# Retention and two expert layers on one core: the first two slots of each layer masked instead of redone behind a branch

## The chip, the cores and the metric

The kernel runs on one core of a Trainium2 chip. The metric is the device time of one execution in microseconds (us); lower is better. Times of a kernel are the median of several runs, beside one profiled execution whose trace is read here. Engines are named as in the profile: PE (TensorE matmuls), DVE (VectorE), ACT (ScalarE), POOL (GpSimd) and SP (the engine that issues most transfers; "SPq" in a row is its queue).

## The reference

Retention (linear attention with decay) over 8 batches, 8 heads, 576 positions, then two layers of experts, each sending each of 4608 rows to one of 8 experts:

```python
ret = scores * Dmat                     # decay mask
x = (ret @ v), rows of 512              # 4608 x 512
# layer 1: normalized logits, argmax; layer 2: x @ w_gate, argmax, and a sigmoid output gate
for e in range(E):
    mask = expert_idx == e
    h = np.maximum(x[mask] @ w1[e], 0.0)           # 512 -> 1024
    out[mask] = gate_w[mask, None] * (h @ w2[e])   # 1024 -> 512
```

## The kernel before, in words

**Buckets and slots.** Each row is scattered by POOL to the bucket of its expert in DRAM (`bk1` for layer 1, `bk2` for layer 2, one stretch of 4608 rows per expert). A layer then goes through *slots* of 128 rows, expert after expert; an expert has at least MIN_SLOTS = 3 slots. `slot_tables` (L155) computes on DVE, from the counts of rows per expert, a table `tix` of integers per slot: where its rows start (Q_START), which weights to fetch next (Q_SRC), whether to fetch them (Q_LD for this layer's next expert, Q_LV for layer 2's first), where to put them (Q_WO), which half of the weight tiles it reads (Q_PO). It also makes `val` and `inv`, masks of the valid rows of each slot. Engines read `tix` into registers with `vload` (L840, a TENSOR_LOAD).

**One slot's work.** `gather` (L846, on SP) loads the 128 rows, `trans_x` (L874 to 876) transposes them on PE and splits them on ACT and DVE into a high and a low part (`xth`, `xtl`), `first` (L885) does 24 matmuls against `w1` (high and low tiles), `relu` (L897, L901), `trans_h` (L909 to 911) transposes and splits the hidden rows, `second` (L921) does 24 matmuls against `w2`, `gated` (L932) scales, and the rows are scattered (L293): in layer 1 to `bk2` after the routing of layer 2 (`trans_g`, `chunk_logits`, `logits` L962, `route2a`, `route2b`), in layer 2 to the output.

**Next weights.** During an expert's slots the next expert's weights come in. `load(s, w)` puts a half of `w1` (w = 1) or `w2` (w = 2), 1 MB, into the tile `raw[w-1]` by a transfer of SP that is carried out only if a register says so (`load_raw`, L332). `step(s, w)` splits `raw` into the high and low weight tiles (`split`: ACT L337, then DVE L338), in the place not in use. In layer 1 `load` issues two transfers into the same tile: this layer's weights, then layer 2's (`v1`, `v2`); the second waits until the first has landed or been skipped.

**The start of a layer.** The table isn't ready when PE could begin. So slots 0 and 1 are taken as expert 0, rows 0 to 255 of its bucket (`load_first`), and run before the table is there (`first(0)`, `first(1, [0, 1])`, ...). If fewer than 256 rows of expert 0 had been scattered by then (`tf`, a flag), the two slots are wrong, and `redo` (in a `tc.Switch` on `fail`, L1051, inside `begin`) fetches the first present expert's weights and does both again. All five engines read the flag (`failed`) and branch. Then `begin` does `load(1, 1)`, `load(1, 2)`, the last masks (`late`), zeroes parts of `bk2` (L309, layer 1 only), `first(1, [3])`, `relu(1)`, `second(0)`, `step(1, 1)`, `load(2, 1)`, `trans_x(2)` and `trans_h(1)`. The program order is written by hand (`manual_schedule`); each engine takes its instructions in that order. From slot 2 on, `period(t, n)` is one slot's program: `step(t-1, 2)`, `load(t, 2)`, `first(t)`, `relu(t)`, `step(t, 1)`, `load(t+1, 1)`, `trans_x(t+1)`, `second(t-1)`, and the rest. A second `Switch`, late in each layer, sets the number of slots.

```python
for case in tc.Switch(fail, 2):     # L1051, in begin
    if case == 1:
        redo(e0)
load(1, 1)
load(1, 2)
```

Of the kernel before, what the change touches and what calls it, by code (L numbers as in the profile page):

```python
# [9 lines left out]
F32 = mybir.dt.float32  # L10
F32R = mybir.dt.float32r
BF16 = mybir.dt.bfloat16
I32 = mybir.dt.int32
# [11 lines left out]
E = 8  # L25
# [4 lines left out]
N_EXACT = NU + E - 1  # L30
NS = NU + E - 1 + (E - 1) * (MIN_SLOTS - 1)
# [26 lines left out]
TI_TOT, TI_E, TI_Q = NQ * NS, NQ * NS + 1, NQ * NS + 2  # L58
NTI = NQ * NS + 3
# [15 lines left out]
def retention_moe_moe(ctx, tc, qh, kth, kh, vh, embT, tau, u1, u2, wg, v1, v2, const, out):  # L75
# [20 lines left out]
    def col(c, n=1):  # L96
# [25 lines left out]
            cp.tile([P, 1], I32, name=f"tf{i}"),  # L122
# [34 lines left out]
    def slot_tables(tab, cum_last, cum_part, psum, seq0):  # L157
# [6 lines left out]
        val, inv, ti, tf = tab  # L164
# [3 lines left out]
        ci, incl, q8, le, y8, t8, t9, pos, cf = (  # L168
            T(n, E, I32 if n == "ci" else F32) for n in "ci incl q8 le y8 t8 t9 pos cf".split()
        )  # L170
        ex, er, ce, nx, loc, sl, r0, sq, jj, nw, f1, pq, hn, rr = (
            T(n, 1, I32 if n == "pq" else F32) for n in "ex er ce nx loc sl r0 sq jj nw f1 pq hn rr".split()
# [6 lines left out]
        def q(i, n=1):  # L179
            return Q[:, i : i + n]  # L180
# [10 lines left out]
        def row(i):  # L191
            return pc[1][:, i * NS : (i + 1) * NS]
# [3 lines left out]
            lambda: ts(out=tf, in0=pc[0][:, E : E + 1], scalar1=float(2 * P), scalar2=None, op0=ALU.is_lt),  # L196
            lambda: ts(out=ci, in0=pc[0][:, :E], scalar1=float(P - 1), scalar2=None, op0=ALU.add),
            lambda: ts(
                out=pos, in0=pc[0][:, :E], scalar1=0.0, scalar2=float(MIN_SLOTS), op0=ALU.is_gt, op1=ALU.mult
            ),  # L200
            lambda: stt(out=y8, in0=pc[0][:, :E], scalar=0.0, in1=iota_n, op0=ALU.is_gt, op1=ALU.mult),
            lambda: ts(out=ci, in0=ci, scalar1=7, scalar2=None, op0=ALU.logical_shift_right),
            lambda: red(out=r0, in_=y8, axis=AX.X, op=ALU.min),
# [4 lines left out]
            lambda: ts(out=r0, in0=r0, scalar1=1000.0, scalar2=float(E - 1), op0=ALU.add, op1=ALU.min),  # L208
            lambda: ts(out=le, in0=incl, scalar1=iota_p, scalar2=0.0, op0=ALU.is_le, op1=ALU.add, accum_out=er),
            lambda: stt(out=q8, in0=incl, scalar=iota_p, in1=incl, op0=ALU.is_le, op1=ALU.mult),  # L210
            lambda: V.tensor_copy(ti[:, TI_E : TI_E + 1], r0[on]),
# [6 lines left out]
            else V.tensor_tensor(out=pq, in0=sq, in1=seq0, op=ALU.add),  # L218
            lambda: stt(
                out=t8, in0=iota_e, scalar=er, in1=pc[0][:, :E], op0=ALU.is_equal, op1=ALU.mult, accum_out=ce  # L220
# [54 lines left out]
            lambda: stt(out=val, in0=row(Q_REM), scalar=iota_p, in1=val, op0=ALU.is_gt, op1=ALU.mult),  # L275
            lambda: ts(out=inv, in0=val, scalar1=-BIG, scalar2=BIG, op0=ALU.mult, op1=ALU.add),
# [3 lines left out]
    def emit(fs):  # L280
        for f in fs:
            f()
# [39 lines left out]
    def load_raw(w, src, ms, cond=None):  # L322

        r = raw[w - 1]
        m = ms[w - 1].rearrange("e k f -> (e k) f")
        if w == 1:
            o, i = r, m[ds(src, 2 * P), :].rearrange("(m p) f -> p m f", p=P)
        else:
            o, i = r.rearrange("p m (j d) -> p m j d", j=2), m[ds(src * 2, 4 * P), :].rearrange(
                "(m j p) d -> p m j d", p=P, j=2  # L330
            )
        nc.sync.dma_start(o, i, **({} if cond is None else {"cond": cond}))  # L332

    def split(w, r, m, off_a, off_v, step):
# [4 lines left out]
        if step:  # L339
            for o in ops:  # L340
                tc.declare_no_dep(o.ins, group="rd", reason="the place written is not the one in use")
                tc.add_to_no_dep_group("wr", o.ins)
        return ops[-1]

    def reads_weights(mm, after=None):

        keep = [after.ins] if after is not None else []
        tc.declare_no_dep(mm.ins, group="wr", keep=keep, reason="the place read is not the one being written")
        if after is not None:
            tc.add_manual_dep(  # L350
                mm.ins,
                after.ins.name,
                mybir.DependencyInfo(mybir.DependencyClass.Sync, mybir.DependencyReason.DATA),
                reason="weights",
            )
        tc.add_to_no_dep_group("rd", mm.ins)
# [467 lines left out]
    def layer(which):  # L824
# [4 lines left out]
        val, inv, ti, tf = tabs[which - 1]  # L829
        ps_h, ps_o, rt, pk, src, po, wo, made = {}, {}, {}, {}, {}, {}, {}, {}  # L830
        L.state = (ps_h, ps_o, rt, pk, src, po, wo, made)
# [12 lines left out]
        def gather(s):  # L844
            r = vload(nc.sync, Q_START * NS + s, E * NT - P)
            nc.sync.dma_start(xrow(s), bk[ds(r, P), :])  # L846

        def load(s, w):

            if w == 1:  # L850
                src[s] = [vload(nc.sync, q * NS + s, mx) for q, mx in ((Q_SRC, E * DM - 2 * P), (Q_LD, 1), (Q_LV, 1))]
            r, ld, lv = src[s]
            load_raw(w, r, ws, ld)
            if g:
                load_raw(w, r, (v1, v2), lv)

        def step(s, w):

            if w == 1:
                wo[s] = [vload(q, Q_WO * NS + s, 3 * FF) for q in (nc.scalar, nc.vector)]  # L860
            for m in range(2):
                made[s, w] = split(w, raw[w - 1], m, *wo[s], True)
# [157 lines left out]
        def start_at(off):  # L1020

            L.base = off if isinstance(off, tuple) else (off,) * 3
            po[0] = po[1] = L.base[2]

        def redo(e0):

            for j in range(2):
                for w in (1, 2):
                    load_raw(w, e0 * DM + j * 2 * P, ws)
                for w in (1, 2):  # L1030
                    for m in range(2):
                        split(w, raw[w - 1], m, L.base[0] + j * FF, L.base[1] + j * FF, False)
            gather(0)
            gather(1)
            trans_x(0, "T", 2)
            first(0)
            relu(0)
            trans_x(1, "T", 2)
            first(1, range(3))
            trans_h(0)  # L1040

        def failed():
            return {e: vload(q, 0, 1, tf) for e, q in everyone.items()}

        def begin(fail, late):


            for s in range(2, 5):
                gather(s)
            e0 = vload(nc.sync, TI_E, E - 1)  # L1050
            for case in tc.Switch(fail, 2):  # L1051
                if case == 1:
                    redo(e0)
            load(1, 1)
            load(1, 2)
# [12 lines left out]
            gated(0)  # L1068
            if not g:
                store(0)  # L1070
            trans_h(1)

        def period(t, n):

            more = g or t < n - 1
            step(t - 1, 2)
            if more:
                load(t, 2)
# [24 lines left out]
            if t + 3 < n:  # L1103
                gather(t + 3)
            if g:
                logits(t - 2)
# [22 lines left out]
        for f in (trans_x, first, relu, trans_h, second, gated, store, trans_g, chunk_logits, logits, route2a, route2b, rank2, failed, begin, run, step, vload, start_at, after):  # L1129
            setattr(L, f.__name__, f)  # L1130
# [28 lines left out]
    fail = L1.failed()  # L1159
    L1.trans_h(0)  # L1160
    emit(tb[ns:-3])
# [4 lines left out]
    for j in range(2):  # L1166
        for m in range(2):
            split(2, raw[j], m, j * FF, j * FF, False)
# [50 lines left out]
    fail = L2.failed()  # L1219
    L2.trans_h(0)  # L1220
    emit(tb[ns:-3])
    L2.first(1, [2])
    L2.begin(fail, tb[-3:])
# [92 lines left out]
```

## Time and profile before

| | us |
|---|---|
| median of 3 runs (1261.49 to 1266.49) | 1264.6 |
| the profiled execution's own time | 1261.13 |
| its span, first to last instruction | 1259.4 |
| PE busy | 1203.2 (96%) |
| DVE busy | 789.4 (63%) |
| ACT busy | 618.5 (49%) |

The span is the stretch that the trace shows; the own time is some 1.7 us longer. A row of the timeline gives start, duration, engine, line, and in brackets the idle time just before it with what ended it. "issue" means that the engine waited for nothing that the profile shows.

### The profile page before, as it was taken

Reading aid. Unit: us, or ns where it says so; the run is one execution under the profiler, and the core shown is the slowest. Engines: PE = TensorE matmul, PEld = TensorE weight load, DVE = VectorE, ACT = ScalarE, POOL = GpSimd, SP = SyncE. Lnnn points to the kernel's source line nnn. Section 1 sums busy time; section 2 is a strip of 40 time slices with the busy share of each in tenths; the row PEclk is TensorE's granted clock in tenths of the full one; section 3 lists DMA queues with packets and bytes.
Section 4 is the critical chain, followed back from the end, with each engine's and each line's share of the span. In section 5 each row is a group of like instructions: output and inputs, shape, how many; then the busy total and the mean of one; then the engine's idle time right before and its main releaser. Section 6 shows DMA issues by size and latency. Waiting matters only on the chain. (4 is left out here: it accounts for less than half of the span.)

```text
span 1259.4 us, 27235 instructions
## 1 busy us (share of the span) xinstructions
PE 1203.2 (96%) x7620; PEld 994.7 (79%) x7620; DVE 789.4 (63%) x1799; ACT 618.5 (49%) x1080; POOL 200.6 (16%) x360
## 2 busy tenths in 40 slices
PE   7998997699999999999999996999999999999997
PEld 6888885588788888888878874888888888888786
DVE  4588675466777667667766764556565655556553
ACT  1454442354555555455555542455555555555453
POOL 3378661000100000010010010000000000000000
PEclk8999997799999999999999998999999999999999
DMA  9997953624343433443443303215144562663110
GB/s 315 269 362 270 329 208 116 178 78 160 112 142 106 157 127 128 142 173 111 166 141 136 123 36 114 100 61 209 59 172 151 200 216 70 213 207 112 35 43 21
DMA packets 89343, 191.02 MB, mean 152 GB/s; under 512 B 9020, under 2 KB 18620, under 8 KB 89152
## 3 DMA queue, kind: packets, MB, share of 16 engines
q1 hardware_dynamic: 78784, 159.16, 38.6%
q0 software_dynamic: 9120, 28.91, 5.8%
q8 instruction: 85, 1.39, 0.5%
q14 instruction: 106, 0.87, 0.2%
q10 hardware_dynamic: 1248, 0.69, 0.2%
HBM read 301.76 MB, written 35.36 MB: 268 GB/s over the span
## 5 line engine op out<-in xcount | busy, mean ns | idle before, releaser
L921 PE MATMUL po<-w2h,hth 128*128 (+1 forms) x624 | 258.4, 414 | 2.4 <-DVE val L275 2.4
L921 PE MATMUL po<-w2h,htl 128*128 (+1 forms) x624 | 247.1, 396 | 0.0
L921 PE MATMUL po<-w2l,hth 128*128 (+1 forms) x624 | 247.0, 396 | 0.0
L338 DVE TENSOR_TENSOR w1l<-raw,w1h 128x1024 f32 x150 | 176.8, 1220 | 83.0 <-ACT w1h L337 83.0
L885 PE MATMUL ph<-w1h,xth 128*128 (+1 forms) x624 | 204.2, 409 | 21.5 <-issue 9.2
L338 DVE TENSOR_TENSOR w2l<-raw,w2h 128x1024 f32 (+1 forms) x154 | 181.7, 1222 | 50.8 <-ACT w2h L337 45.8
L911 DVE TENSOR_TENSOR htl<-pt,hth 128x512 fp32r<-128x512 f32 x156 | 100.5, 686 | 178.1 <-ACT hth L910 177.6
L885 PE MATMUL ph<-w1l,xth 128*128 (+1 forms) x624 | 196.4, 396 | 0.6 <-DVEq L1051 0.6
L885 PE MATMUL ph<-w1h,xtl 128*128 (+1 forms) x624 | 195.0, 394 | 0.0
L337 ACT CAST w1h<-raw 128x1024 f32 x150 | 149.9, 1047 | 63.7 <-DMA raw<-in_v_dram 56.4
L337 ACT CAST w2h<-raw 128x1024 f32 (+1 forms) x154 | 153.9, 1054 | 11.8 <-issue 6.5
L932 ACT ACTIVATE orow<-po,xg 128x512 f32<-128x512 f32 x74 | 50.9, 687 | 195.0 <-PE po L921 192.4
L885 PEld LDWEIGHTS ph<-w1h,xth 128*128 128x128 f32 x624 | 112.8, 192 | 42.6 <-issue 14.7
L921 PEld LDWEIGHTS po<-w2h,hth 128*128 128x128 f32 x624 | 118.3, 190 | 33.4 <-issue 9.7
L885 PEld LDWEIGHTS ph<-w1l,xth 128*128 128x128 f32 x624 | 118.7, 190 | 27.2 <-DVEq L1051 1.3
L921 PEld LDWEIGHTS po<-w2h,htl 128*128 128x128 f32 x624 | 118.0, 189 | 28.1
L885 PEld LDWEIGHTS ph<-w1h,xtl 128*128 128x128 f32 x624 | 118.8, 190 | 26.6
L921 PEld LDWEIGHTS po<-w2l,hth 128*128 128x128 f32 x624 | 118.7, 190 | 22.7
L293 POOL DMA_INDIRECT bk<-orow,bix x39 | 38.2, 980 | 504.9 <-DVE orow L1016 318.2
L897 ACT ACTIVATE hs<-ph 128x512 f32<-128x512 f32 x78 | 46.5, 597 | 132.8 <-PE ph L885 132.8
L293 POOL DMA_INDIRECT out_dram<-orow,oix x39 | 37.9, 972 | 457.6 <-ACT orow L932 425.9
L910 ACT CAST hth<-pt 128x512 fp32r<-128x512 f32 x156 | 83.6, 589 | 8.8 <-PE pt L909 8.8
(205 smaller groups left out, 1398.2 us busy)
## 6 DMA issues: line engine op xcount, KB each, us to landing
raw<-in_v_dram SPq DMA_DIRECT2D x150, 1024.0 KB
raw<-in_w_dram SPq DMA_DIRECT2D x76, 1024.0 KB
xg<-bk SPq DMA_DIRECT2D x74, 264.0 KB
qt<-in_qh_dram SPq DMA_DIRECT2D x36, 256.0 KB
vr<-in_vh_dram SPq DMA_DIRECT2D x36, 256.0 KB
kr<-in_kh_dram SPq DMA_DIRECT2D x36, 256.0 KB
kt<-in_kth_dram SPq DMA_DIRECT2D x34, 256.0 KB
bk<-z SPq DMA_DIRECT2D x18, 264.0 KB
```

The costliest lines, as they stand in the source:

```text
L293: i = nc.gpsimd.indirect_dma_start(out=table, out_offset=bass.IndirectOffsetOnAxis(ap=ix, axis=0), in_=rows, in_offset=None, bounds_check= ...
L337: ops = [nc.scalar.copy(at(h[m], off_a, 0, FF), r[:, m, :])]
L338: ops.append(nc.vector.tensor_sub(at(l[m], off_v, 0, FF), r[:, m, :], at(h[m], off_v, 0, FF)))
L885: mm = nc.tensor.matmul(ps_h[s][i], st[:, k, :], at(w1[n][k % 2], po[s], k // 2 * FF + i * 512, 512), start=(k == 0 and n == 0 and st is x ...
L897: nc.scalar.activation(hsb[:, 0:512], ph[0], AF.Relu)
L910: nc.scalar.copy(hth[s % 2][:, h, :], ps)
L911: nc.vector.tensor_sub(htl[s % 2][:, h, :], ps, hth[s % 2][:, h, :])
L921: mm = nc.tensor.matmul(ps, st[:, f, :], at(w2[n][a % 2], po[s], a // 2 * FF + b * 512, 512), start=(f == 0 and n == 0 and st is hh), stop ...
L932: nc.scalar.activation(o[:, 0:DM], ps_o.pop(s), AF.Copy, scale=x[:, DM : DM + 1])
```

## The change

The branch and `redo` are gone. Instead the number of rows of expert 0 that were missing from the first two slots, d0 = max(0, 256 - count at that time), is computed; `val` masks slots 0 and 1 down to what was there, expert 0's count is raised by d0, and its later slots start d0 rows earlier. Expert 0 gets at least 4 slots instead of 3 (`MIN_SLOTS + 1`), and its fetch of next weights runs one slot later (`lj` for `loc`): `begin` has no `step(1, 1)`, and loads for slot 2 rather than for slot 1. In layer 1 the transfers of layer 2's weights (`load_v`) stand apart from `load`, later in SP's order, and no longer wait for the other transfer into the same tile. The slot table has room for 60 slots instead of 57.

```diff
-            lambda: ts(out=tf, in0=pc[0][:, E : E + 1], scalar1=float(2 * P), scalar2=None, op0=ALU.is_lt),
+            lambda: ts(
+                out=d0, in0=pc[0][:, E : E + 1], scalar1=-1.0, scalar2=float(2 * P), op0=ALU.mult, op1=ALU.add
             ),
+            lambda: ts(out=d0, in0=d0, scalar1=0.0, scalar2=None, op0=ALU.max),
...
+            lambda: ts(out=cf[:, 0:1], in0=cf[:, 0:1], scalar1=float(MIN_SLOTS + 1), scalar2=None, op0=ALU.max),
...
+            lambda: ts(out=lj, in0=er, scalar1=1.0, scalar2=-float(P), op0=ALU.is_lt, op1=ALU.mult),
+            lambda: V.tensor_tensor(out=lj, in0=lj, in1=loc, op=ALU.add),
...
+            lambda: ts(out=val[:, 0:1], in0=iota_p, scalar1=d0, scalar2=float(2 * P), op0=ALU.add, op1=ALU.is_lt),
+            lambda: ts(out=val[:, 1:2], in0=iota_p, scalar1=d0, scalar2=float(P), op0=ALU.add, op1=ALU.is_lt),
...
-            load_raw(w, r, ws, ld)
-            if g:
-                load_raw(w, r, (v1, v2), lv)
+            loads[s, w] = [load_raw(w, src[s][0], ws, src[s][1])]
+
+        def load_v(s, w, apart=True):
+
+
+            got = load_raw(w, src[s][0], (v1, v2), src[s][2])
+            if apart:
+                tc.add_to_no_dep_group("raw", loads[s, w][0].ins)
+                tc.declare_no_dep(got.ins, group="raw", reason="one of the two at most is carried out")
+            loads[s, w].append(got)
...
-        def begin(fail, late):
+        def begin(late):
 
 
             for s in range(2, 5):
                 gather(s)
-            e0 = vload(nc.sync, TI_E, E - 1)
-            for case in tc.Switch(fail, 2):
-                if case == 1:
-                    redo(e0)
-            load(1, 1)
-            load(1, 2)
+            load(2, 1)
+            load(2, 2)
+            if g:
+                load_v(2, 1)
+                load_v(2, 2)
             emit(late)
...
-            step(1, 1)
-            load(2, 1)
             trans_x(2)
...
-            step(t - 1, 2)
-            if more:
-                load(t, 2)
+            if t > 2:
+                step(t - 1, 2)
+                if more:
+                    load(t, 2)
+                    if g and t == n - 1:
+                        load_v(t, 2, False)
...
                 load(t + 1, 1)
+                if g and t > 2:
+                    load_v(t, 2)
...
                 gather(t + 3)
+            if g and t + 1 < n:
+                load_v(t + 1, 1)
...
-    L1.begin(fail, tb[-3:])
-    base2 = tuple(L1.vload(e, TI_Q, 2 * FF) for e in (nc.scalar, nc.vector, nc.tensor))
+    L1.begin(tb[-5:])
+    base2 = L1.vload(nc.tensor, TI_Q, 2 * FF)
```

What moves, in the engines' own order (rows of the compiled program; `raw_74` and `raw_75` are raw[0] and raw[1], `in_w` the layer's weights, `in_v` layer 2's, `xs`, `xg` gathered rows; in brackets the semaphores an instruction waits for).

ACT, layer 1, from the branch's end into slot 1. Before:

```order
L1312 UNCONDITIONAL_BRANCH
L897 ACTIVATE hs<-ph_1_0_3149 128x512 [waits PE_49,Activation_49]
L840 TENSOR_LOAD tix [waits DVE_49]
L840 ISA x2
L337 ISA
L337 COPY w1h_70<-raw_74 128x1024 [waits DMAHW3_49,DVE_49]
L337 ISA
L337 COPY w1h_71<-raw_74 128x1024 [waits DVE_49]
L875 CAST xth_2939<-px_2_3553 128x512 [waits DVE_49,PE_49]
L932 ACTIVATE orow_3263<-po_0_3474,xs_86 128x512 [waits DMASW7_49,DMASW6_49,DMAHW5_49,DMASW3_49,DMAHW6_49,DMASW2_49,PE_49]
L910 CAST hth_2945<-pt_1_0_3568 128x512 [waits PE_49]
```

And now:

```order
L345 CAST w2h_3203<-raw_75 128x1024
L908 ACTIVATE hs<-ph_1_0_3155 128x512 [waits PE_49,Activation_49]
L886 CAST xth_2937<-px_2_3341 128x512 [waits PE_49]
L943 ACTIVATE orow_3224<-po_0_3313,xs_86 128x512 [waits DMASW6_49,DMASW3_49,DMASW7_49,DMASW2_49,DMAHW5_49,DVE_49,PE_49]
L921 CAST hth_2943<-pt_1_0_3356 128x512 [waits PE_49]
L921 CAST hth_2943<-pt_1_1_3363 128x512 [waits PE_49]
L908 ACTIVATE hs<-ph_2_0_3408 128x512 [waits PE_49,Activation_49]
L845 TENSOR_LOAD tix [waits DVE_49]
L845 ISA x2
L345 ISA
L345 COPY w1h_70<-raw_74 128x1024 [waits DMAHW4_49,DMAHW2_49]
```

The split of `w1` from `raw[0]`, which waits for a transfer (DMAHW), stood ahead of `xth`, `orow` and `hth`; now it stands behind them and behind slot 2's `relu`.

SP, layer 1, the loads of `begin`. Before (behind the branch and three `vload`s):

```order
L332 ISA
L332 DMA raw_74<-in_w_dram 128x2x1024 [waits DMAHW2_49,DMAHW4_49,DVE_49,Activation_49]
L332 ISA
L332 DMA raw_74<-in_v_dram 128x2x1024 [waits DMAHW3_49,DMAHW2_49]
L332 ISA
L332 DMA raw_75<-in_w_dram 128x4x512 [waits DMAHW5_49,DVE_49,Activation_49]
L332 ISA
L332 DMA raw_75<-in_v_dram 128x4x512 [waits DMAHW4_49]
L309 DMA bk_69<-z 512x1x132 [waits DMAHW6_49]
```

And now:

```order
L338 ISA
L338 DMA raw_74<-in_w_dram 128x2x1024 [waits DMAHW2_49,DVE_49]
L338 ISA
L338 DMA raw_75<-in_w_dram 128x4x512 [waits DMAHW3_49,DVE_49]
L338 ISA
L338 DMA raw_74<-in_v_dram 128x2x1024 [waits DMAHW4_49]
L338 ISA
L338 DMA raw_75<-in_v_dram 128x4x512 [waits DMAHW5_49]
L315 DMA bk_69<-z 512x1x132 [waits DMAHW6_49]
```

The two `in_w` loads stand next to each other; between them stood the wait of the `in_v` transfer for the first.

SP, layer 1, in the periods. Before, `load(3, 1)` with its `in_v`, `gather(5)`, and `load(3, 2)` with its `in_v`:

```order
L332 ISA
L332 DMA raw_74<-in_w_dram 128x2x1024 [waits DMAHW3_49,DMAHW0_49,DVE_49]
L332 ISA
L332 DMA raw_74<-in_v_dram 128x2x1024 [waits DMAHW4_49,DMAHW3_49]
L840 TENSOR_LOAD tix
L840 ISA x2
L846 ISA
L846 DMA xg_3260<-bk_68 128x528 [waits DMAHW5_49]
L332 ISA
L332 DMA raw_75<-in_w_dram 128x4x512 [waits DMAHW6_49,DMAHW2_49,DVE_49]
L332 ISA
L332 DMA raw_75<-in_v_dram 128x4x512 [waits DMAHW6_49]
```

And now `load(4, 1)`, `load_v(3, 2)`, `gather(6)`, `load_v(4, 1)`, `load(4, 2)`:

```order
L338 ISA
L338 DMA raw_74<-in_w_dram 128x2x1024 [waits DMAHW3_49,DMAHW1_49,DVE_49]
L338 ISA
L338 DMA raw_75<-in_v_dram 128x4x512 [waits DMAHW4_49]
L845 TENSOR_LOAD tix
L845 ISA x2
L851 ISA
L851 DMA xg_3222<-bk_68 128x528 [waits DMAHW5_49,Activation_49,Pool_49]
L338 ISA
L338 DMA raw_74<-in_v_dram 128x2x1024 [waits DMAHW6_49]
L338 ISA
L338 DMA raw_75<-in_w_dram 128x4x512 [waits DMAHW7_49,DMAHW4_49,DVE_49]
```

Each `in_v` transfer now follows its `in_w` at a distance, the one for `raw[1]` about half a period later than it did.

## Rows read from the trace of the kernel before

**Rows 1.** The page: busy time of PE, its share and number of instructions; and the granted TensorE clock in 40 equal slices of the span, in tenths.

```profile
PE 1203.2 (96%) x7620; PEld 994.7 (79%) x7620; DVE 789.4 (63%) x1799; ACT 618.5 (49%) x1080; POOL 200.6 (16%) x360
...
PEclk8999997799999999999999998999999999999999
```

**Rows 2.** The waits of PE over the whole span: who was waited for, us in total, times, longest.

```profile
PE pl L962 <- ACT lsb L959: 9.5, 3, 8.8
PE ph L885 <- issue: 9.2, 2, 5.1
PE ph L885 <- ACT hth L910: 8.6, 2, 5.3
```

**Rows 3.** The timeline of PE at the start of layer 1: start, duration, what, and in brackets the idle time before it.

```profile
199.26 0.63 PE L885 MATMUL ph<-w1h,xtl 128*128 128x512 f32 x2
204.04 1.22 PE L885 MATMUL ph<-w1h,xth 128*128 128x512 f32 x2 [4.16 <-issue]
...
210.39 0.77 PE L921 MATMUL po<-w2h,hth 128*128 128x512 f32 x1 [2.43 <-DVE val L275]
...
216.08 0.43 PE L921 MATMUL po<-w2l,hth 128*128 128x512 f32 x1
...
223.37 1.19 PE L885 MATMUL ph<-w1h,xth 128*128 x2 [3.21 <-ACT hth L910]
...
228.07 0.62 PE L885 MATMUL ph<-w1l,xth 128*128 x2
228.53 0.61 PE L885 MATMUL ph<-w1h,xtl 128*128 x2
...
230.34 0.60 PE L944 MATMUL pg<-ident,orow 128*128 128x128 f32 x4
...
237.11 0.40 PE L921 MATMUL po<-w2h,htl 128*128 128x512 f32 x1
246.28 0.61 PE L962 MATMUL pl<-cs,lsb 128*128 128x16 f32 x2 [8.77 <-ACT lsb L959]
...
248.33 1.20 PE L885 MATMUL ph<-w1h,xth 128*128 x2
...
254.80 0.60 PE L944 MATMUL pg<-ident,orow 128*128 128x128 f32 x4
```

**Rows 4.** The timelines of DVE, ACT and SP's queue in the same stretch (for SP: issue of a transfer; x3 and x9 are merged, with the time from the first to the last issue).

```profile
201.15 4.63 DVE L338 TENSOR_TENSOR w2l<-raw,w2h 128x1024 fp32r<-128x1024 f32 x4
209.66 0.28 DVE L274 TENSOR_SCALAR val<-tabs,cs 128x57 f32<-128x57 f32 x1 [3.88 <-issue]
...
219.79 1.99 ACT L337 CAST w1h<-raw 128x1024 f32 x2 [11.55 <-DMA raw<-in_v_dram]
...
243.59 1.99 ACT L337 CAST w1h<-raw 128x1024 f32 x2 [12.62 <-DMA raw<-in_v_dram]
...
204.41 2.84 SPq L846 DMA_DIRECT2D xg<-bk  x3
214.60 0.41 SPq L332 DMA_DIRECT2D raw<-in_w_dram  x1
219.64 0.10 SPq L332 DMA_DIRECT2D raw<-in_v_dram  x1
...
225.36 8.55 SPq L309 DMA_DIRECT2D bk<-z  x9
236.66 0.39 SPq L332 DMA_DIRECT2D raw<-in_w_dram  x1
243.45 0.08 SPq L332 DMA_DIRECT2D raw<-in_v_dram  x1
```

**Rows 5.** The timelines of PE, DVE, ACT and SP's queue at the start of layer 2.

```profile
769.46 1.22 PE L885 MATMUL ph<-w1h,xth 128*128 x2 [5.06 <-issue]
...
772.18 0.56 PE L921 MATMUL po<-w2h,hth 128*128 x1
...
776.54 0.60 PE L874 MATMUL px<-ident,xg 128*128 128x128 f32 x4
...
784.77 1.19 PE L885 MATMUL ph<-w1h,xth 128*128 x2 [5.35 <-ACT hth L910]
...
792.59 0.60 PE L874 MATMUL px<-ident,xg 128*128 128x128 f32 x4
...
761.10 0.15 DVE L244 TENSOR_TENSOR st_Q<-st_f,st_Q 128x1 f32<-128x1 f32 x1
...
781.18 1.99 ACT L337 CAST w1h<-raw 128x1024 f32 x2 [8.54 <-DMA raw<-in_v_dram]
...
765.66 3.60 SPq L846 DMA_DIRECT2D xg<-bk  x3
776.01 20.89 SPq L332 DMA_DIRECT2D raw<-in_v_dram  x5
```

**Rows 6.** Slots and their length: the page's groups of the first half of `relu` (one per slot run) and of the scatters of layer 1 (one per slot), with busy time, mean ns, idle before; and two gathers of neighbouring slots in SP's timeline.

```profile
L293 POOL DMA_INDIRECT bk<-orow,bix x39 | 38.2, 980 | 504.9 <-DVE orow L1016 318.2
...
L897 ACT ACTIVATE hs<-ph 128x512 f32<-128x512 f32 x78 | 46.5, 597 | 132.8 <-PE ph L885 132.8
...
811.89 0.35 SPq L846 DMA_DIRECT2D xg<-bk  x1
824.27 0.35 SPq L846 DMA_DIRECT2D xg<-bk  x1
```

More of the change, by code (lines that the diff above doesn't have):

```diff
@@ L29 @@
 MIN_SLOTS = 3
[L30 to L31 removed]
+NS = NU + E - 1 + (E - 1) * (MIN_SLOTS - 1) + 3
 BIG = 262144.0
@@ L157, in slot_tables @@
     def slot_tables(tab, cum_last, cum_part, psum, seq0):
-        val, inv, ti, tf = tab
+        val, inv, ti = tab
         V = nc.vector
@@ L167, in slot_tables @@
         T = lambda n, k, dt=F32: cp.tile([P, k], dt, tag="st_" + n, bufs=2, name="st_" + n)
[L168 to L172 removed]
+        ci, incl, q8, le, y8, t8, t9, pos, cf, cc = (
+            T(n, E, I32 if n == "ci" else F32) for n in "ci incl q8 le y8 t8 t9 pos cf cc".split()
+        )
+        ex, er, ce, nx, loc, sl, sq, jj, nw, f1, pq, hn, rr, d0, de, lj = (
+            T(n, 1, I32 if n == "pq" else F32) for n in "ex er ce nx loc sl sq jj nw f1 pq hn rr d0 de lj".split()
         )
@@ L331, in load_raw, with split @@
             )
-        nc.sync.dma_start(o, i, **({} if cond is None else {"cond": cond}))
-    def split(w, r, m, off_a, off_v, step):
+        return nc.sync.dma_start(o, i, cond=cond)
+    SYNC = mybir.DependencyInfo(mybir.DependencyClass.Sync, mybir.DependencyReason.DATA)
+    def split(w, r, m, off_a, off_v, loads=()):
         h, l = (w1, w2)[w - 1]
@@ L338, in split @@
         ops.append(nc.vector.tensor_sub(at(l[m], off_v, 0, FF), r[:, m, :], at(h[m], off_v, 0, FF)))
-        if step:
+        for i in loads:
+            tc.add_manual_dep(ops[0].ins, i.ins.name, SYNC, reason="raw weights")
+        if loads:
             for o in ops:
@@ L349, in reads_weights @@
         if after is not None:
[L350 to L355, printed above, removed]
+            tc.add_manual_dep(mm.ins, after.ins.name, SYNC, reason="weights")
         tc.add_to_no_dep_group("rd", mm.ins)
@@ L828, in layer @@
         bk, ws = (bk1, (u1, u2)) if g else (bk2, (v1, v2))
-        val, inv, ti, tf = tabs[which - 1]
-        ps_h, ps_o, rt, pk, src, po, wo, made = {}, {}, {}, {}, {}, {}, {}, {}
-        L.state = (ps_h, ps_o, rt, pk, src, po, wo, made)
+        val, inv, ti = tabs[which - 1]
+        ps_h, ps_o, rt, pk, src, po, wo, made, loads = {}, {}, {}, {}, {}, {}, {}, {}, {}
+        L.state = (ps_h, ps_o, rt, pk, src, po, wo, made, loads)
         def out_rows(s):
@@ L861, in step @@
             for m in range(2):
-                made[s, w] = split(w, raw[w - 1], m, *wo[s], True)
+                made[s, w] = split(w, raw[w - 1], m, *wo[s], loads[s, w])
         def after(other, s):
@@ L1020, in start_at @@
         def start_at(off):
[L1022 to L1043, printed above, removed]
-        def begin(fail, late):
+            po[0] = po[1] = off
+        def begin(late):
             for s in range(2, 5):
                 gather(s)
-            e0 = vload(nc.sync, TI_E, E - 1)
-            for case in tc.Switch(fail, 2):
-                if case == 1:
-                    redo(e0)
-            load(1, 1)
-            load(1, 2)
+            load(2, 1)
[3 more added lines that the diff above has]
+                load_v(2, 2)
             emit(late)
@@ L1127, in run @@
                 end(n)
-        for f in (trans_x, first, relu, trans_h, second, gated, store, trans_g, chunk_logits, logits, route2a, route2b, rank2, failed, begin, run, step, vload, start_at, after):
+        for f in (trans_x, first, relu, trans_h, second, gated, store, trans_g, chunk_logits, logits, route2a, route2b, rank2, begin, run, step, vload, start_at, after):
             setattr(L, f.__name__, f)
@@ L1158, in retention_moe_moe @@
     L1.first(1, [0, 1], SPEC)
-    fail = L1.failed()
     L1.trans_h(0)
-    emit(tb[ns:-3])
+    emit(tb[ns:-5])
     L1.first(1, [2])
@@ L1218, in retention_moe_moe @@
     L2.first(1, [0, 1], SPEC)
-    fail = L2.failed()
     L2.trans_h(0)
-    emit(tb[ns:-3])
+    emit(tb[ns:-5])
     L2.first(1, [2])
-    L2.begin(fail, tb[-3:])
+    L2.begin(tb[-5:])
     L2.run(finish)
```

31 lines of the change are left out of this document (15 added, 16 removed).

## The prediction

> **What bounds the kernel now.** I read the page first. PE is busy for 1203.2 us, so it sets the time, and only what PE waits for, or does at a low clock, can be won. The granted clock in 40 slices falls in three places: the first slice, slices 6 and 7 (189 to 252 us, 0.7) and slice 24 (756 to 787 us, 0.8) [rows 1]. The last two are the starts of the two layers. The list of PE's waits says the same: three kinds cost 27.3 us, and nearly all of that is in five waits [rows 2], which the timelines place: 4.16, 3.21 and 8.77 us at layer 1's start [rows 3], 5.06 and 5.35 us at layer 2's [rows 5]. A sixth, 2.43 us for `val`, belongs to the first group [rows 3].
>
> The timelines of the other engines tell whose they are. At 199.9 us PE has done its part of slot 1 and sits 4.16 us for nothing that the profile shows; DVE does the same for 3.88 us after its last `w2l` split at 205.78 us [rows 3, 4]. In the program the branch on `fail` stands in just these two places. PE's 5.06 us of "issue" in layer 2 is the same place [rows 5]. The other three waits end on ACT, and ACT itself had waited 11.55, 12.62 and 8.54 us for `raw` before splitting `w1` [rows 4, 5]: `step(1, 1)` and `step(2, 1)` stand in ACT's order ahead of the `xth`, `hth` and `lsb` that PE needs, and SP issued the loads late (214.60, 236.66 and 776.01 us) [rows 4, 5].
>
> **Layer 1, term by term.** *The branch.* PE's six matmuls `first(1, [3])` can follow at 199.9 and end near 201.3, at 0.46 us a pair [rows 3]. `second(0)` then cannot start, because its PSUM bank is the one that held the tables, which `val` still reads, and `val` comes after the four `w2l` splits, which end at 205.78 [rows 4]. So what is late next is DVE: `val` right behind the splits instead of at 209.66, two operations of some 0.3 us, and `second(0)` at about 206.6 instead of 210.39 [rows 3, 4]. The change lengthens DVE's table chain by five small operations (0.15 us at most each [rows 5], so 0 to 0.75 us) and drops its read of the flag. The two further operations on single columns of `val` come behind the ones that free the bank. The gain is 3.0 to 3.9 us; I take **3.6**. PE keeps a wait of about 5 us there and the slow stretch after it, up to 216.08 in the trace [rows 3]. I leave that stretch as long as it is.
>
> *The two waits on ACT.* With no `step(1, 1)` nothing that waits for a transfer stands before `xth` in slot 1; 3.21 us go. `step(2, 1)` now finds `raw` loaded from `begin`; 8.77 us go. Together **12.0** [rows 3].
>
> *The clock.* `first` is 12 pairs of matmuls, 5.5 us at 0.46 us a pair. After the 3.21 us wait it took 6.97 us (223.37 to 230.34), after the 8.77 us wait 6.47 us (248.33 to 254.80) [rows 3]. Without those waits the surplus goes: **2.4**. Layer 1 gives 18.0.
>
> Is the cover there? SP issues its third gather at 207.25 and three register loads took it 2.75 us (from the last zero write at 233.91 to 236.66), so `load(2, 1)` goes out near 210 instead of 214.60, and `load(2, 2)` right behind it. One load alone took 5.04 us (214.60 to 219.64), one amid the zero writes 6.79 us (236.66 to 243.45) [rows 4]: two at once, with the zero writes behind them, land between 216 and 220. They are wanted when `first(2)` ends: 206.6, plus 9.8 us of PE work (210.39 to 223.37 less the wait), plus 5.5, which is 221.9 [rows 3]. `load(3, 1)` waits for DVE's split of `raw[0]` and the register loads, so it goes out at 226 to 228 and lands by 233 to 235. It is wanted at the end of `first(3)`, about 236: 7.2 us of PE work (230.34 to 237.51), some 1.4 for the small matmuls and transposes and 5.5 for `first(3)` after 221.9 [rows 3]. Cover of 1 to 3 us, and PE would feel a late split only when `logits` wants `lsb`, some 3 us later still.
>
> **Layer 2.** 5.06 us of the branch go. Here DVE has no splits, so PE runs on into `second(0)`; `first(1, [3])` took 2.72 us (769.46 to 772.18) and needs 1.4 warm, which gives 1.3 more; the five table operations lie on the path and I take 0.4 back [rows 5]. The 5.35 us wait goes with `step(1, 1)`, and `first(2)`, 7.82 us (784.77 to 792.59), comes down to 5.5, so 2.3 [rows 5]. Sum **13.6**. Cover: the gather of slot 2 goes out at about 766.1 and `trans_x(2)` wants it 4.4 us (772.18 to 776.54) into `second(0)`, at about 770.6. The gathers show no landing; a quarter of the 1 MB that took 5.04 us should land in time, and at the worst 0.6 us are lost. `load(2, 1)` goes out 2.75 us after the third gather (769.26), at 772.0, and lands 5.2 us later as it did (776.01 to 781.18) at 777.2; `first(2)` ends at 779.1 [rows 4, 5].
>
> **Edits with no cost or gain.** The splits left out (two on ACT and two on DVE per weight and layer) ran beside PE otherwise. Unchaining the second transfer of layer 2's weights, and moving it behind `gather`, shortens SP's queue, but the five waits named leave PE almost nothing to win in the periods [rows 2]. The transfer into `raw[1]` goes out half a period later, about 9.5 us into 12.4 [rows 6]; it is carried out only in three slots of the last expert, and would land some 2 us into the next period, where ACT has 5.5 us before `relu` and needs 2. Bounds: 0 to 3 us lost. One read of `base2` instead of three: nothing.
>
> **The sum.** 18.0 + 13.6 = 31.6 us. Against the profiled execution, 1261.1 us, that is 1229.5 us. The median of the runs shown lies 3.5 us above that execution, which would give 1233.0. I say **1231 us**, between the two.
>
> **Rivals.** *A: the loads become the wait.* If `load(3, 1)`, behind nine zero writes some of which now wait for the loads before them, lands after about 239 us, ACT again holds `lsb`, and 8.77 us and the 0.95 us of clock stay: 1239. For it: 6.79 us beside the zero writes against 5.04 alone [rows 4]. Against: it goes out some 9 us earlier. The Trainium skill ("DMA: Bandwidth & Descriptors", Issuing engines are not separate DMA queues) says that all transfers interleave on the same 16 DMA engines, so unchained loads would share them rather than overlap for free; the 6.79 us agrees with that.
>
> *B: the "issue" waits are not the branch's.* Something else that stays in place, such as the register loads or the jump over code, would keep the 3.6 us and the 5.06 + 1.3 - 0.4 us: 1239. Against it: DVE sits 3.88 us at the same place of its own program, six microseconds after PE [rows 3, 4]. The Trainium skill ("Advanced Engine Details and Errata", Control Flow Timing) puts a compare-and-branch at about 108 ns; by that figure, an estimate, the removed branch would give back 0.1 us per layer and the time would be this rival's. No row shows a branch that short: the trace has 3.88 to 5.06 us at the three places.
>
> *C: slower, by extra slots.* The masking pays for missing rows with further slots, each 12.4 us (811.89 to 824.27) [rows 6]. Expert 0 can gain up to 256 rows, so two slots, and its minimum is one higher. Three extra slots over the two layers eat the gain; two in each layer would give 1229.5 + 4 x 12.4 = 1279. Against it: the test is the same as the flag's, and the flag was not set in either layer, since `relu` ran 78 times, which is 39 slots in layer 1 and 39 in layer 2 with no slot twice [rows 6]. So d0 is 0. The minimum of four bites only if expert 0 has under four slots; the reference's own routing gives it 590 and 851 rows, five and seven slots.
>
> *D: the change does little.* If conditional transfers into one tile waited for each other anyhow, that part would be as before; it carries nothing in my sum.
>
> **How the numbers follow.** My forecast 0.81 (1225 to 1237), A 0.07, B 0.07, C 0.03, and 0.02 for one extra slot in each layer or other losses that end near 1255. Within the forecast, the slow stretch left in layer 1 could be shorter by up to 2.6 us or longer by as much, DVE's chain is worth 1 us, the late `raw[1]` transfers 0 to 3, the choice of base 3.5. The range, **1223 to 1243**, takes in A and B, with the 3.5 us of the median on top. About 0.5% (6.3 us) is what a measurement of this kernel can tell from no change: faster 0.95, same 0.02, slower 0.03.
>
> **What would show it.** Right: no "issue" wait of PE in 195 to 230 and 755 to 790 us; one wait for `val` of about 5 us in layer 1 near 201; no wait for `hth` or `lsb` over 1 us; `second(0)` near 206.6 and 766.4; 39 slots in each layer; ACT's first split of next weights behind slot 2's `relu` without a wait for `raw`. Wrong: ACT waiting for `raw` in slots 2 or 3 (A), "issue" waits still there (B), 40 or more slots (C), or waits in later periods that before had none.

## The result and the profile after

| | before | after |
|---|---|---|
| median, us | 1263.1 (4 runs, 1261.49 to 1266.49) | 1227.66 (4 runs, 1225.77 to 1228.02) |
| the profiled execution's own time, us | 1261.13 | 1225.77 |
| its span, us | 1259.4 | 1223.9 |
| ratio of the times | | 0.9713 (95%: 0.9688 to 0.9738) |

By the medians the kernel became 35.4 us faster; the prediction was 31.6 us against the profiled execution, and 1231 us as the time. The page of the kernel after, for [rows 1] and [rows 6]:

```profile
PE 1193.0 (97%) x7620; PEld 988.4 (81%) x7620; DVE 775.7 (63%) x1805; ACT 611.9 (50%) x1072; POOL 203.0 (17%) x360
PEclk9999998999999999999999999999999999999999
...
L299 POOL DMA_INDIRECT bk<-orow,bix x39 | 38.3, 982 | 487.9 <-DVE orow L1027 412.2
L908 ACT ACTIVATE hs<-ph 128x512 f32<-128x512 f32 x78 | 46.6, 597 | 121.3 <-PE ph L896 117.6
```

PE runs the same 7620 matmuls in 10.2 us less. Of the low slices at the two layers' starts only one, at 0.8, is left. The slots are as many as before: 78 `relu`, and 39 scatters in layer 1. The timeline of PE at the start of layer 1, for [rows 3]:

```profile
197.46 1.07 PE L188 MATMUL tabs<-st_X,ones 128*128 128x480 f32 x2 [1.33 <-DVE tix L255]
...
205.60 0.76 PE L932 MATMUL po<-w2h,hth 128*128 128x512 f32 x1 [4.31 <-DVE val L279]
...
210.00 0.63 PE L932 MATMUL po<-w2l,hth 128*128 128x512 f32 x1
210.43 0.52 PE L932 MATMUL po<-w2h,htl 128*128 128x512 f32 x1
210.79 0.39 PE L932 MATMUL po<-w2h,hth 128*128 128x512 f32 x1
211.01 0.40 PE L932 MATMUL po<-w2l,hth 128*128 128x512 f32 x1
...
214.80 0.71 PE L896 MATMUL ph<-w1h,xth 128*128 x2
...
220.38 0.60 PE L955 MATMUL pg<-ident,orow 128*128 128x128 f32 x4
...
227.41 0.29 PE L973 MATMUL pl<-cs,lsb 128*128 128x16 f32 x2
228.37 0.71 PE L896 MATMUL ph<-w1h,xth 128*128 x2
...
233.96 0.60 PE L955 MATMUL pg<-ident,orow 128*128 128x128 f32 x4
```

Three of layer 1's four waits are gone; the one for `val` stays, 1.9 us longer than before, and ends 4.8 us earlier. A wait of 1.33 us for the table chain has come ahead of the tables, where it was 0.17 us before. DVE, ACT and SP's queue in that stretch, for [rows 4]:

```profile
200.32 4.63 DVE L346 TENSOR_TENSOR w2l<-raw,w2h 128x1024 fp32r<-128x1024 f32 x4
204.87 0.27 DVE L278 TENSOR_SCALAR val<-tabs,cs 128x60 f32<-128x60 f32 x1
```

```profile
212.81 0.59 ACT L886 CAST xth<-px 128x512 fp32r<-128x512 f32 x1 [11.05 <-PE px L885]
...
221.37 2.00 ACT L345 CAST w1h<-raw 128x1024 f32 x2 [0.36 <-DVE hs L912]
...
234.74 2.00 ACT L345 CAST w1h<-raw 128x1024 f32 x2 [0.16 <-ACT hs L908]
```

```profile
202.87 2.87 SPq L851 DMA_DIRECT2D xg<-bk  x3
207.81 1.12 SPq L338 DMA_DIRECT2D raw<-in_w_dram  x2
209.23 0.49 SPq L338 DMA_DIRECT2D raw<-in_v_dram  x2
209.76 12.02 SPq L315 DMA_DIRECT2D bk<-z  x9
224.84 0.39 SPq L338 DMA_DIRECT2D raw<-in_w_dram  x1
```

DVE takes `val` right behind the splits. ACT waits for PE at `xth`, and in this stretch never for `raw`. (It does three times at the end of layer 1, 3.7 us together, and PE waits for none of these.) PE at the start of layer 2, for [rows 5]:

```profile
741.26 1.07 PE L188 MATMUL tabs<-st_X,ones 128*128 128x480 f32 x2 [1.33 <-DVE st_X L249]
741.80 0.99 PE L896 MATMUL ph<-w1h,xth 128*128 x2
...
744.93 0.40 PE L932 MATMUL po<-w2h,hth 128*128 x1
...
751.76 0.71 PE L896 MATMUL ph<-w1h,xth 128*128 x2
...
757.30 0.60 PE L885 MATMUL px<-ident,xg 128*128 128x128 f32 x4
```

No wait is left here but 1.33 us for the table chain. From the last of these rows to the end it is 466.6 us, against 466.8 before: the rest of layer 2 gave nothing.

### The profile page after: what moved, and what is told of

Same layout as the page of the kernel before. It is cut to its first block, busy times and chain, and to the rows that moved or that the text cites. A ratio compares the mean times of both kernels' runs of the same rounds, so it can differ in the third digit from the quotient of the medians.

```text
span 1223.9 us, 27034 instructions
## 1 busy us (share of the span) xinstructions
PE 1193.0 (97%) x7620; PEld 988.4 (81%) x7620; DVE 775.7 (63%) x1805; ACT 611.9 (50%) x1072; POOL 203.0 (17%) x360
## 4 chain that ended last, share of the span: by engine, by line
PE 89%; DVE 3%; DMA 2%; POOL 2%; issue 2%; ACT 1%; another core or an unknown queue 1%; SPq 0%; ACTq 0%; POOLq 0%; DVEq 0%
PE po L932 36%; PE ph L896 34%; PE pt L920 5%; PE px L885 3%; PE tp L619 2%; PE sc L486 2%; PE xp L549 2%; PE xp L536 2%; PE pg L955 1%; PE pl L962 1%; PE sps L586 1%; DMA bk<-rows,ps 1%; DMA gv<-in_const_dram 0%; DMA kt<-in_kth_dram 0%
## 5 line engine op out<-in xcount | busy, mean ns | idle before, releaser
L346 DVE TENSOR_TENSOR w2l<-raw,w2h 128x1024 f32 (+1 forms) x150 | 176.9, 1222 | 46.9 <-ACT w2h L345 41.8
L896 PE MATMUL ph<-w1h,xth 128*128 (+1 forms) x624 | 201.4, 404 | 3.5 <-DVE t L988 1.8
L346 DVE TENSOR_TENSOR w1l<-raw,w1h 128x1024 f32 x146 | 171.9, 1219 | 34.9 <-ACT w1h L345 34.9
L896 PE MATMUL ph<-w1l,xth 128*128 (+1 forms) x624 | 193.7, 392 | 0.0
L345 ACT CAST w2h<-raw 128x1024 f32 (+1 forms) x150 | 149.9, 1054 | 8.1 <-issue 7.9
L345 ACT CAST w1h<-raw 128x1024 f32 x146 | 146.0, 1048 | 13.4 <-DMA raw<-in_v_dram 3.7
L912 DVE TENSOR_SCALAR hs<-ph 128x512 f32<-128x512 f32 x76 | 52.3, 688 | 56.4 <-PE ph L896 56.4
```

Source lines behind the costliest of these rows:

```text
L896: mm = nc.tensor.matmul(ps_h[s][i], st[:, k, :], at(w1[n][k % 2], po[s], k // 2 * FF + i * 512, 512), start=(k == 0 and n == 0 and st is x ...
L912: nc.vector.tensor_scalar(out=hsb[:, 512:], in0=ph[1], scalar1=0.0, scalar2=None, op0=ALU.max)
```

## Experiments

Each time stands beside runs of the kernel before on the same chip (medians 1261.4 to 1262.6 us).

**The edits one by one.** First the kernel before without the flag's reads, `redo` and the branch, which this input does not need:

```diff
-            for case in tc.Switch(fail, 2):
-                if case == 1:
-                    redo(e0)
...
-    fail = L1.failed()
...
-    fail = L2.failed()
...
```

> The kernel before without the Switch, redo and the reads of the flag; all else as before (it would be wrong where the flag is set, which it is not with these inputs). Theory: only the branch's part comes, 4.8 us in layer 1 and 6.5 in layer 2 as the changed trace shows them, while the waits for raw stay: hth about 2 us in layer 1 and 6 in layer 2 (loads go out earlier, but PE is earlier too), lsb about 9. 1250 to 1253 us. Rival (the branch also holds SP's loads back, so most of the gain comes from it): the hth and lsb waits shrink to under 2 us together, 1238 to 1242 us.

Measured: 1248.43 us, ratio 0.9893 (0.9866 to 0.9920), 13.7 us off. Its waits of PE in 190 to 830 us (who waited for whom, us in total, times, longest):

```profile
PE pl L962 <- ACT lsb L959: 9.0, 1, 9.0
PE ph L885 <- ACT hth L910: 8.0, 2, 5.9
PE po L921 <- DVE val L275: 4.3, 1, 4.3
```

That is 1.6 us below the theory's range and 6 above the rival's. The "issue" waits are gone, the waits on ACT stay about as they were. So the former went with the branch and its flag reads, while the other register loads stayed: rival B falls. The reads and the branch went together, but the traces keep them apart: the reads stand ahead of `trans_h(0)`, where DVE's `htl` starts 1.10 us behind layer 1's tables with them (before, and the runs with the chain undone alone and with the empty branch, below) and 0.24 or 0.25 us without (here and in after), whereas the long waits stand at the branch's own place. Then the shift by a slot alone, branch and chain of the loads kept:

```diff
...
-            load(1, 1)
-            load(1, 2)
+            load(2, 1)
+            load(2, 2)
...
-            step(1, 1)
-            load(2, 1)
...
```

> The kernel before with the split of next weights one slot later for expert 0 (minimum of 4 slots, no step(1,1), begin loads for slot 2), the branch and the chained loads kept. Theory: the waits for hth and lsb and the slow clock behind them go (3.2 + 8.8 + 5.4, and some 5.5 of clock), the two issue waits stay at 4 to 5 us: 1238 to 1243 us. Rival (the shift only moves the wait to the next slot, since SP's chained loads and zero writes are still behind): an lsb wait of 5 to 9 us in slot 3 of layer 1, 1246 to 1251 us.

Measured: 1241.90 us, ratio 0.9835 (0.9804 to 0.9867), 20.2 us off, with these waits in the same stretch:

```profile
PE ph L888 <- issue: 11.9, 2, 8.1
PE po L924 <- DVE val L278: 2.3, 1, 2.3
...
PE pl L965 <- ACT lsb L962: 0.6, 1, 0.6
```

The theory's range holds it. The picture is the reverse of the last one: "issue" stays, the waits on ACT are gone but for 0.6 us, and it is the larger half. Then only the transfers of layer 2's weights, moved and unchained (`load_v`), in the kernel before:

> The kernel before with only the second transfers moved and unchained as in the change; branch and step(1,1) kept. Theory: in layer 1 load(2,1) goes out some 7 us earlier (about 229 instead of 236.7), so the 8.8 us wait for lsb falls to 1 to 2 us, the others stay: 1253 to 1257 us; layer 2 as before. Rival (unchaining does nothing where the loads are late for other reasons): 1261 to 1265 us with the 8.8 us wait unchanged.

Measured: 1255.42 us, ratio 0.9956 (0.9933 to 0.9979), 6.7 us off. The theory's range holds it: PE's wait for `lsb` fell to 4.0 us, the others stayed. And the kernel after with the chain put back:

```diff
             loads[s, w] = [load_raw(w, src[s][0], ws, src[s][1])]
+            if g:
+                loads[s, w].append(load_raw(w, src[s][0], (v1, v2), src[s][2]))
...
```

> The changed kernel with the transfers of layer 2's weights issued right behind each load again, the second waiting for the first. Theory (the branch and the shifted split carry the gain, unchaining only adds cover): SP gets through begin some 9 us later (load(2,2) about 213 us, zero writes 218 to 227, load(3,1) out at 227 to 230 and landed near 236), but the split of raw[0] is wanted at 234 and PE asks for its followers only at 241: 1228 to 1230 us, no wait of PE for lsb over 1 us. Rival (unchaining is needed for the 8.8 us wait to go): lsb is waited for again in slot 2 or 3, 1233 to 1237 us.

Measured: 1226.70 us, ratio 0.9725 (0.9695 to 0.9755): no difference from after. `load(3, 1)` goes out later there, at 227.70 us, and ACT waits for it:

```profile
235.71 2.00 ACT L345 CAST w1h<-raw 128x1024 f32 x2 [3.02 <-DMA raw<-in_v_dram]
```

PE shows no wait for `lsb` all the same: the shift's slack takes the 3 us. The parts alone add to 13.7 + 20.2 + 6.7 = 40.6 us, over the 35.4, because the shift and the unchaining remove the same wait for `lsb`: unchaining, worth 6.7 us alone, adds nothing on top of the other two.

**What the branch's price hangs on.** In the kernel after, the flag, its five reads and a `Switch` came back, with one memset as its body:

```diff
...
+            for case in tc.Switch(fail, 2):
+                if case == 1:
+                    nc.vector.memset(dum, 0.0)
...
```

> The changed kernel with the flag, its five reads and a Switch on it put back at the same place, but with one 1-column memset as its body instead of redo. Theory (the branch itself holds each engine for some 4 to 5 us, however little code it jumps over: before, DVE jumped over 15 rows and waited 3.88 us, PE over some 50 and waited 4.16): PE waits for issue 4 to 5 us at each layer's start again, val in layer 1 comes some 4 us later: 1238 to 1241 us. Rival (the cost is the jump over redo's code): no issue wait over 0.5 us, 1227 to 1230 us. By the Trainium skill's 108 ns for a compare-and-branch (Advanced Engine Details and Errata, Control Flow Timing) it would be the rival's time too.

Measured: 1242.54 us, ratio 0.9850 (0.9823 to 0.9876), 13 to 15 us slower than after (1227.66 us, and 1229.64 us in a second set of runs, below), and 1.5 over the theory's range. PE's and DVE's rows in both layers:

```profile
204.48 1.22 PE L898 MATMUL ph<-w1h,xth 128*128 128x512 f32 x2 [2.40 <-issue]
211.58 0.76 PE L934 MATMUL po<-w2h,hth 128*128 128x512 f32 x1 [4.18 <-DVE val L281]
...
755.28 1.22 PE L898 MATMUL ph<-w1h,xth 128*128 x2 [4.66 <-issue]
758.00 0.63 PE L934 MATMUL po<-w2h,hth 128*128 x1
...
1152.93 1.19 PE L898 MATMUL ph<-w1h,xth 128*128 x2 [3.10 <-issue]
```

```profile
210.84 0.28 DVE L280 TENSOR_SCALAR val<-tabs,cs 128x60 f32<-128x60 f32 x1 [3.62 <-issue]
...
755.56 0.28 DVE L280 TENSOR_SCALAR val<-tabs,cs 128x60 f32<-128x60 f32 x1 [4.84 <-issue]
```

An empty branch costs about as much as the one with `redo`: its body's length is not the price. Against the spans of after, layer 1's start lost 4.6 us between table and `second(0)`, and layer 2's 6.2. The last of PE's rows, 3.10 us at 1153 us, stands at the second `Switch` of layer 2, ahead of slot 33, which every kernel here keeps. After waits there too, 1.32 us at 1137.10 us, put down to DVE's `htl`; so this wait became 1.8 us longer. One more view bears on the cause, the packets of the queues that carry instructions around layer 2's branch. Before (761 to 770 us), the empty branch (748 to 755.3 us) and after (741 to 750 us):

```profile
q14 instruction: 10, 0.08, 4.9%
q8 instruction: 2, 0.03, 2.5%
```

```profile
q14 instruction: 7, 0.06, 5.0%
q8 instruction: 2, 0.03, 3.8%
```

```profile
q14 instruction: 2, 0.02, 0.6%
```

Where there is a branch, 9 to 12 packets of instructions are fetched in that stretch, without one, 2. In layer 1 it is 12 before (198 to 210 us), 10 with the empty branch (199 to 211 us) and none in after (197 to 206 us). The Trainium skill ("Runtime: NRT & Kernel Launch", Instruction fetch mechanics) says that a taken branch whose target lies outside the pages at hand stalls the engine until the page is fetched; the packets agree with that. They do not prove it: at the second `Switch` of layer 2, 6 packets come with the empty branch (1146 to 1153 us) and 6 in after (1133 to 1140 us), and PE waits 3.10 us in one and 1.32 in the other. PE's wait at the removed branch was 2.40 to 8.06 us over places and kernels (the longest in the shift alone), and what sets its size stays open.

**When rows are missing.** The two ways of paying for them were set against each other: after with d0 forced to 256 (slots 0 and 1 fully masked), and before with its flag forced (`redo` taken in both layers).

> The changed kernel with d0 set to 256 in both layers, as if no row of expert 0 had been there: slots 0 and 1 masked whole, two more slots for expert 0 in each layer. Theory: 41 slots a layer instead of 39, 4 x 12.4 = 49.6 us more than the changed kernel: 1277 us, with relu 82 times and nothing else longer. Rival (the further slots also bring waits, or the last Switch costs more): over 1285 us.

> The kernel before with the flag set in both layers, so that redo runs. Theory: per layer two rounds of two 1 MB loads, eight splits on ACT and DVE, and the two slots' first halves on PE again, in one chain: 25 to 35 us per layer at a clock that falls, so 1310 to 1335 us, more than the masks cost when all rows are missing. Rival (the redo overlaps with its own loads): 15 to 20 us a layer, 1293 to 1303 us.

Measured, one run each: 1281.02 and 1303.47 us: the first between the two theories, the second at the top of the rival's range. The four extra slots cost 53.4 us, 13.3 each where rival C took 12.4 (layer 2's slots stand 12.4 us apart, layer 1's 13.6); `redo` cost 41.5 us over before, with two waits put down to the reload of the rows in place of those for `hth`, `lsb` and "issue":

```profile
PE px L874 <- DMA xs<-bk: 52.3, 2, 27.3
```

So C's mechanism exists and its price is right within a tenth, but even with all rows missing the masked kernel was 22 us faster than the one that redoes them.

**The wait that is left.** In layer 1, `val`'s two operations that free the PSUM bank were put ahead of the `w2l` splits:

```diff
-    emit(tb[ns:-5])
+    emit(tb[ns : ns + 2] + tb[-5:-3])
...
-    L1.begin(tb[-5:])
+    L1.begin(tb[-3:] + tb[ns + 2 : -5])
```

> The changed kernel with the two operations on val that free the PSUM bank put ahead of the w2l splits in layer 1, and the parity of layer 2's weights and the rest of the masks behind them. Theory: second(0) of layer 1 no longer waits 4.3 us for val behind four splits; it starts near 201.4 instead of 205.6, the clock does not fall there (2.4 us of the stretch 205.6 to 210.8 come back), and a gather or a split may cost 1 us of it: 5 to 6.6 us less than the changed kernel, 1221 to 1223 us. Rival (the w2l splits bind there, not val): second(0) waits for w2l instead, 0 to 2 us gained.

Measured: 1226.70 us, ratio 0.9724 (0.9702 to 0.9746), not to be told from after: the rival's time, though not by its wait for `w2l`. PE's wait for `val` is gone and `second(0)` starts at 200.2 us, but new waits stand behind it, of PE and of ACT:

```profile
PE pl L973 <- ACT lsb L970: 1.6, 1, 1.6
...
PE px L885 <- DMA xg<-bk: 1.3, 1, 1.3
```

```profile
ACT w1h L345 <- DMA raw<-in_w_dram: 5.5, 1, 5.5
```

PE is early, and the third load is not: it went out at 224.60 us, behind the nine zero writes. So these were moved ahead, with `val` first (e9) and alone (e10), and after was run once more beside them:

```diff
-            if g:
-                for i in range(3):
-                    zero_heads(bk2, i)
...
+    for i in range(3):
+        zero_heads(bk2, i)
     L1.first(1, [0, 1], SPEC)
...
```

> The kernel after with val's two operations ahead of the w2 splits (as in e6), and the nine zero writes of the second layer's token table issued about 27 us earlier, behind the load of xs, while SP is idle, instead of between the slot-2 loads and load(3,1). Theory (e6 lost its gain again to load(3,1), which stood behind the nine writes): load(3,1) is issued before 217 us instead of 224.6, ACT's 5.5 us wait for the raw weights and PE's 1.6 us for lsb go, layer 2's tables come at about 735 us, and the time is 1221 to 1224 us. Rival (the loads are late for another reason, the bandwidth of three 1 MB loads, or the gain goes into the next wait, W's tables or the gather): the time stays at 1226 to 1228 us.

> The kernel after with the nine zero writes moved alone, val left where it is. In the kernel after no engine that TensorE follows waits for load(3,1), so both theories expect no change: 1226 to 1229 us. Below 1224 us the writes would have cost something that the waits do not show; above 1231 us they would disturb the first layer's scatters at 176 to 188 us.

> The changed kernel itself, beside the two others on the same chip: 1226 to 1229 us. It is the base against which the two are read.

Measured: 1228.63, 1233.84 and 1229.64 us, ratios 0.9733 (0.9716 to 0.9751), 0.9764 (0.9744 to 0.9784) and 0.9739 (0.9720 to 0.9758). My theory was half right. From layer 1's tables to layer 2's it is 543.8 and 544.7 us in the two traces of after, 542.3 with `val` first, and 539.0 with both, where ACT no longer waits for that load. But the writes now go out at 177 us, and ACT's wait for a scatter of token rows in 170 to 210 us grew from 3.7 us in after's second trace (first row) to 7.9 and 8.3 (e9, e10):

```profile
ACT rows L629 <- DMA bk<-rows,ps: 3.7, 1, 3.7
```

```profile
ACT rows L629 <- DMA bk<-rows,ps: 7.9, 2, 6.4
```

```profile
ACT rows L629 <- DMA bk<-rows,ps: 8.3, 1, 8.3
```

From 177 to 190 us the mean busy share of the transfer engines is 0.31 and 0.36 in the two traces of after and 1.07, that is without a break, in e9; PE is busy for 8.8 us of it instead of 10.9 and 11.2. Alone the writes cost 4.2 us by the medians; with `val` first they give back what was won. The last run put them into units 18 to 20 of the attention stage:

```diff
+            if 18 <= u < 21:
+                zero_heads(bk2, u - 18)
...
```

> As e9, but the nine zero writes go out three at a time in the attention stage's units 18 to 20, at about 103 to 116 us, where the transfers are lightest, instead of at 177 us. Theory (e9's first layer gained 5 us over the kernel after, and lost it ahead of the layer, since at 177 us the writes kept the token rows' scatters and so ACT's rows buffer waiting 8 us instead of 4): ACT's wait for the scatter is 4 us again, the first layer keeps e9's gain, and the time is 1222 to 1225 us. Rival (the order of SP is not what decides, the spread of the attention stage from run to run is): 1227 to 1230 us.

Measured: 1228.70 us, ratio 0.9732 (0.9719 to 0.9746): the rival's time. The scatter's wait is back at 3.7 us, and layer 1 keeps its gain (540.3 us from tables to tables). But in 100 to 150 us, where the writes now lie, PE is busy 44.0 us, against 47.8 and 46.8 in the traces of after, and waits for a unit's own load:

```profile
PE sc L486 <- DMA kt<-in_kth_dram: 1.8, 1, 1.8
```

These writes found no free place in any of the three tried. Layer 1's tables come at 197.5 and 202.5 us in the two traces of after, so a spread of 5 us ahead of the layer also hides gains of this size; that the last run's writes cost what layer 1 gained is argued from PE's busy time, not shown by the medians. No version beat after by more than its interval.

## Why the prediction was right, and where its sizes were off

All of it comes from differences of the timelines, [rows 3, 5] against the rows of after, and from two rows of before, PE at the tables of layer 1 and of layer 2:

```profile
197.46 1.03 PE L189 MATMUL tabs<-st_X,ones 128*128 128x456 f32 x2 [0.17 <-DVE tix L251]
...
761.97 1.03 PE L189 MATMUL tabs<-st_X,ones 128*128 128x456 f32 x2 [0.56 <-DVE st_X L245]
```

| Term | predicted, us | measured, us |
|---|---|---|
| layer 1: branch, `second(0)` earlier | 3.6 | 4.79 (210.39 to 205.60) |
| layer 1: wait of 3.21, and slow stretch | 3.21 | 3.78 |
| layer 1: `first(2)` at full clock | 1.47 | 1.39 (6.97 to 5.58) |
| layer 1: wait of 8.77 | 8.77 | 8.91 |
| layer 1: from `logits` to the end of `first(3)` | 0.97 | 1.97 (8.52 to 6.55) |
| layer 2: branch, with the cold matmuls behind it | 5.96 | 6.54 |
| layer 2: wait of 5.35 | 5.35 | 5.76 |
| layer 2: `first(2)` at full clock | 2.3 | 2.28 (7.82 to 5.54) |
| the rest of both layers | 0 | 0.07 |
| sum | 31.6 | 35.5 |

The forecast lay 3.3 us above the median: 3.8 from the terms, and 0.5 back from the base between profile and median that it was laid on. Layer 1's tables come at 197.46 us in both traces, so nothing of the sum came from ahead of them. That is luck: they came at 202.50 us in after's second trace, and the five table operations ahead of them, priced at 0 to 0.75 us, can't be read from this sum.

*The mechanism held, place by place.* The waits that went are those named, each in its place. The one expected to stay did (about 5 us forecast, 4.3 measured), and `val` runs where the text put it, right behind the splits. In layer 2 PE ran on into `second(0)`.

*The cover held, with less to spare than the numbers say.* The slot-2 loads went out at 207.8 and 208.6 us (forecast near 210), `load(3, 1)` at 224.84 (226 to 228), and ACT waited for none. Rival A did not happen; with PE 5 us earlier (`val` first) its beginning shows, 5.5 us of ACT's and 1.6 of PE's.

*Layer 1's branch was mis-sized by 1.2 us.* I took 3.6 from `val` alone. DVE also began its splits earlier (200.32 for 201.15), since its own read of the flag stood ahead of them; I had named that read and given it no price. It is the 0.85 us by which `htl` starts later in every trace with the read than in those without (1.10 against 0.24 or 0.25 us behind the tables).

*The clock was mis-sized by about 1.6 us.* "I leave that stretch as long as it is" cost 0.6: `second(0)`'s matmuls start 0.43 us apart at the lower of the clock's two levels (1.2 GHz; 0.50 granted from 205.6 to 210.7 us) and 0.23 apart at the upper (2.4 GHz; 1.00 from 210.8 us). They change over at 210.8 us, 5.2 us after the first of them; before it was at 216.1, after 5.7 us [rows 3]. And the surplus after the 8.77 us wait was taken for `first(3)` alone, while `logits` and the transposes ahead of it ran at the low clock too (0.50 granted from 246.3 to 248.3 us): 2.05 us from `logits` to `first(3)` before [rows 3], 0.96 after, at 1.00.

*Layer 2 was mis-sized by 1.0 us,* 0.6 of it at the branch. The 0.4 that I took back for the five table operations does not fall in that stretch but ahead of it, among "the rest". There they cost what the upper bound said: PE's wait at the tables grew from 0.56 to 1.33 us. It hardly shows in the sum, because the transposes ahead of the tables came 21.48 us earlier, though layer 1's start had given 20.84. Nearly all of this 0.64 came at one place, a further wait of PE for `lsb` in layer 1, 0.58 us at 316.90 us, behind 4.47 us that ACT waited for `raw`; after has none. It lies between the 9.5 and the 8.8 us of [rows 2], and the prediction gave the periods nothing in its sum. That "the rest" came to 0.07 is these two cancelling.

*The price of the branch has no single figure.* Removing it alone, with its flag reads, gave 13.7 us, and putting an empty one back cost 13 to 15. The Trainium skill ("Advanced Engine Details and Errata", Control Flow Timing) gives about 108 ns for a compare-and-branch; by that figure, an estimate, removing it would have given 0.1 us per layer. Where page and trace differ, the trace decided here.

*The edit without a price.* Unchaining was rated at nothing beside the shift, and it is nothing (1226.70 against 1227.66 us). The experiment says why: it removes a wait that the shift has already made harmless.

## What to carry to other kernels

A wait of a few us before PE can cost more than its length: behind the waits of 3 to 9 us here PE ran at the low clock, transposes and small matmuls too, so read the surplus of everything up to the next wait. Look at every engine's own gap at the same place of its program: "issue" on PE and DVE six microseconds apart was one branch. And ask of each removed wait whether a second edit of the change removes it too; parts measured alone then add to more than the whole.

## What the runs showed of the hardware

At a branch whose body isn't run PE sat 2.4 to 8.1 us, with `redo` as its body or one memset, and its flag's read took DVE another 0.85 us. Nine writes of 264 KB (2.4 MB) cost 4.2 us when they alone were moved to 177 us, where SP had issued nothing (1233.84 against 1229.64 us): the mean busy share of the transfer engines then was 1.1 to 1.2 from 182 to 192 us, and ACT waited 8.3 us for a scatter instead of 3.7. A queue's idle time is not the transfers' room.
